# Five edits to an adaLN, long-convolution and SwiGLU block: norm rows at the gate, five-step statistics, paced spectrum loads, 100-column matmuls, 64-row pairs in the last row block

## The chip, the core and the metric

The kernel runs on one core of a Trainium2 chip. The metric is device time in microseconds (us) of one launch, lower is better; runs are compared by their median. Engines are named as in the profile: PE (matmuls) and PEld (its weight loads), DVE (vector), ACT (scalar), POOL (GpSimd), SP (the queue that issues nearly all DMAs).

## What is computed

Sequence 2048, width 576, hidden width 4608, everything stored in bf16. Six modulation rows come from one conditioning row. A first layernorm of `q` is modulated and multiplied by a long convolution of `k_shift * v` along the sequence; the result goes back onto the residual. A second layernorm feeds a SwiGLU.

```
mod = silu(c) @ w_mod                      # sa, ca, ga, sb, cb, gb
h   = layernorm(q) * (1 + ca) + sa
kv  = (4-tap shift of k) * v
y   = fftconv(kv, ssm_k)[:2048] + kv * ssm_D
x   = q + ga * (h * y)
h   = layernorm(x) * (1 + cb) + sb
out = x + gb * ((silu(h @ w1) * (h @ w3)) @ w2)
```

## The kernel before, in words

**Tiling.** The sequence is cut into 8 blocks of 256 rows (`s`, two rows to a partition) for the convolution, and into 4 row blocks of 512 rows (`r`) for the SwiGLU. The convolution of a block is done with short spectra: `x_spectrum(s)` makes the spectrum X of block s from `kv` (matmuls, copied out of PSUM by ACT), `w_spectrum` and `v_block` make the filter spectra V, and `pair(X, V, s)` multiplies two of them into an accumulator on DVE (L405 for the first, L410 and L412 for the others, each on 128x3456 elements). Later blocks need pairs with all earlier X and V; those that no longer fit are spilled to DRAM and fetched again by `get` (L430 to L434; three buffers for X, four for V). `inverse` (L539) turns the accumulator back into rows, `residual` adds it, and `outcome` makes the second norm. `turn_all` (L571) transposes the rows into `h2T`, the operand of the SwiGLU.

**First norm.** `gate_stats(s)` lets ACT make sums and sums of squares (L440, a Copy and a Square, each with an accumulator read), and `ln_scales` (L450 to L461) turns them into a scale and a shift with six small POOL operations: L455 mean, L456 variance term, L457 mean squared, L458 difference, L459 power -0.5, L460 shift. `gate_rows(s)` (L493 to L502) is two ACT activations of 128x576 that write `hg`, the normed rows; `gate(s)` is the modulation of `hg` on DVE (L511, L513). In `conv(s0)`, which handles blocks s0 and s0+1, `gate_rows(s0)` stands ahead of `x_spectrum(s0)`, and `gate(s0)` comes at the end of what runs beside that spectrum (`beside`): `v_block(s1)`, `load_kv(s1)`, `gate_stats(s1)`, up to two pairs, then the gate.

**SwiGLU.** `stream(r, ...)` runs over 36 tiles f of 128 hidden columns, in 9 chunks `fc` of four. For each f there are a gate product (w1) and an up product (w3) over 576 = 4*128 + 64 rows: eight matmuls of 128 rows (L916) and two of 64 rows (L927), one for w1 on partitions 0 to 63 and one for w3 on 64 to 127, issued side by side. ACT then applies Silu (L935) and copies the up product (L937), DVE multiplies them into `h3` (L938). Tiles are grouped by two, in the last row block by four, so that the 64-row matmuls of a group stand together. `load_w13` (L867 the 512 KB slabs, L868 the 64 KB ones) fills one of two buffers. `down(r)` multiplies `h3` with w2 (L982, loads at L973), DVE scales and adds to the residual (L999, L1000).

**Order.** The convolution of blocks 2r+2 and 2r+3 is a generator whose steps carry a cost; `advance` takes steps while `stream` and `down` of row block r are written out, so that DVE works on the convolution beside PE's SwiGLU. The instructions are then ordered within each engine by a scheduler that takes what it thinks is ready, in order of priority, unless an edge fixes the order. `behind(engine)` is such an edge: what is traced inside it is issued after the engine's last instruction so far. `get` has none. The first block is written out by hand (`first_block`, with `in_order` for DVE, ACT and PE). There `mod_columns` (L248) makes the columns of cb and sb with 60 matmuls of one output column each, and `warm` (L626) runs matmuls whose result nobody reads.

Of the kernel before, what the change touches and what calls it, by code (L numbers as in the profile page):

```python
# [2 lines left out]

# [19 lines left out]
NF = F // P  # L23
RB = 512
NRB = S // RB
FC = 4
# [6 lines left out]
N1 = 24  # L33
SPLIT = 2
EPS = 1e-5


def _ap(t, offset, dims):
# [5 lines left out]
class _Kernel:  # L44
    def __init__(self, ctx, tc, q, k, v, shift_k, ssm_k, ssm_D, w1, w3, w2, c, w_mod, out):
        self.tc, self.nc = tc, tc.nc
        self.q, self.k, self.v = q, k, v
        self.shift_k, self.ssm_k, self.ssm_D = shift_k, ssm_k, ssm_D
        self.w1, self.w3, self.w2, self.c, self.w_mod, self.out = w1, w3, w2, c, w_mod, out
        pool = lambda name, **kw: ctx.enter_context(tc.tile_pool(name=name, **kw))  # L50
        self.const = pool("const", bufs=1)
        self.psum = pool("psum", bufs=4, space=bass.MemoryType.PSUM)
        self.dram = pool("spill", bufs=1, space=bass.MemoryType.DRAM)
        self.spec = pool("spec", bufs=4)
        self.wprev = pool("wprev", bufs=2)
        self.prod = pool("prod", bufs=1)
        self.acc = pool("acc", bufs=1)
        self.ld = pool("ld", bufs=1)
        self.kvp = pool("kvp", bufs=1)
        self.x1p = pool("x1p", bufs=4)  # L60
        self.lnp = pool("lnp", bufs=1)
        self.small = pool("small", bufs=4)
        self.hp = pool("hp", bufs=4)
        self.xo, self.hg, self.accs, self.l1 = {}, {}, {}, {}
        self.X, self.V, self.Wl = {}, {}, {}
        self.w13, self.kept = {}, {}

    def ps(self, shape=(P, 2, 512), dtype=F32):
        return self.psum.tile(list(shape), dtype, name="ps", tag="ps")
# [2 lines left out]
    def setup(self):  # L72
        nc, const = self.nc, self.const
        nc.scalar.preload_act_table(ACT.Silu)
        self.ident = const.tile([P, P], BF16, name="ident")
        self.npi = const.tile([P, 1], F32, name="npi")
# [159 lines left out]
    def mod_columns(self):  # L236

        nc = self.nc
        w5 = self.wm[:, 0:5 * 6 * D].rearrange("p (a d) -> p a d", a=5)
        ps = self.ps()  # L240
        for i, m in enumerate((4, 3)):
            for j in range(6):
                lo = min(P * j, 512)
                n = P if j < 4 else 64
                out = ps[0:n, i, j:j + 1] if j < 5 else ps[64:P, i, 4:5]
                for ct in range(5):
                    k = P if ct < 4 else 64
                    nc.tensor.matmul(out, w5[0:k, ct, m * D + lo:m * D + lo + n],  # L248
                                     self.crep[0:k, ct, 0:1], start=(ct == 0), stop=(ct == 4))
        nc.scalar.activation(self.cbcol[:], ps[:, 0, 0:5], ACT.Copy, bias=1.0)  # L250
        nc.scalar.copy(self.sbcol[:], ps[:, 1, 0:5])


    def load_kv(self, s, between=None):
# [175 lines left out]
    def get(self, which, i):  # L430
        t = self.spec.tile([P, 6, D], BF16, name=which, tag=which, bufs=3 if which == "X" else 4)
        src = self.Xd if which == "X" else self.Vd
        self.nc.sync.dma_start(t[:].rearrange("p a d -> p (a d)"), src[i])
        return t  # L434

    def ln_sums(self, src, i, ssum, ssq, col=None):
        col = i if col is None else col
        for func, out in ((ACT.Copy, ssum), (ACT.Square, ssq)):
            junk = self.lnp.tile([P, D], BF16, name="junk", tag="junk")
            self.nc.scalar.activation(junk[:], src[:, i, :], func, accum_out=out[:, col:col + 1])  # L440

    def ln_stats(self, src, name):

# [6 lines left out]
    def ln_scales(self, ssum, ssq, name):  # L450
        small = self.small
        n = ssum.shape[-1]
        mean, var, rstd, nmr = [small.tile([P, n], F32, name=name + k, tag=f"ln{k}{n}") for k in "mvrn"]
        e = self.nc.gpsimd
        e.tensor_single_scalar(mean[:], ssum[:], -1.0 / D, op=ALU.mult)  # L455
        e.tensor_scalar(var[:], ssq[:], 1.0 / D, EPS, op0=ALU.mult, op1=ALU.add)  # L456
        e.tensor_mul(rstd[:], mean[:], mean[:])  # L457
        e.tensor_sub(var[:], var[:], rstd[:])  # L458
        e.tensor_tensor(rstd[:], var[:], self.neghalf[:, 0:n], op=ALU.pow)  # L459
        e.tensor_mul(nmr[:], mean[:], rstd[:])  # L460
        return rstd, nmr  # L461

    def quick_stats(self, src, name):
# [329 lines left out]
    def conv(self, s0):  # L793
# [24 lines left out]
            if s0 == 2:  # L818
                yield from self.pair(self.X[0], self.V[s0], s0)
        yield from self.mix(filters(), old())  # L820
        self.gate_rows(s0)
        X0, V0 = self.old_x(0, s0), self.old_v(0, s0)

        def beside():
            yield from self.v_block(s1)
            with self.behind(self.nc.sync):
                self.load_kv(s1)
            yield from self.gate_stats(s1)
            if s0 > 2:
                yield from self.pair(X0, self.V[s0], s0)  # L830
            self.X1 = self.old_x(1, s0)
            yield from self.pair(X0, self.V[s1], s1)
            yield from self.gate(s0)
        yield from self.mix(self.x_spectrum(s0), beside())
        yield from self.x_sums(s0)
# [45 lines left out]
    def stream(self, r, jobs, rate, size, finish=False):  # L881
# [64 lines left out]
        for k in range(0, len(items), size):  # L946
# [13 lines left out]
            for m in late:  # L960
                full(m, False)
                hide(m)

    def down(self, r, rate):
        nc = self.nc
        for h in range(2):
# [4 lines left out]
            for f0 in range(0, NF, W2C):  # L971
                w = _ap(self.w2m, (h * NF + f0) // W2C % NW2 * W2C * H, [[H, W2C], [1, H]])
# [8 lines left out]
                for f, t in order:  # L981
                    nc.tensor.matmul(acc[t],  # L982
                                     self.h3[:, f0 + f, t * P:(t + 1) * P], w[:, f, :],
                                     start=(f0 + f == 0), stop=(f0 + f == NF - 1))
# [51 lines left out]
    def row_blocks(self, n1):  # L1036
        for r in range(NRB):
            cost = 0
            if r + 1 < NRB:
                s0 = 2 * r + 2  # L1040
# [4 lines left out]
            rate = cost / time  # L1045
# [9 lines left out]
            else:  # L1055
                spills = {1: (self.keep_x, 1), 2: (self.keep_v, 0), 4: (self.keep_v, 1)} if r == 1 else {}
                jobs = [(fc, 0, RB, (r + fc) % 2, (lambda f, i: lambda: f(i))(*spills[fc]) if fc in spills else None)
                        for fc in range(NF // FC)]
            self.stream(r, jobs, rate, 4 if r == NRB - 1 else 2)
            self.down(r, rate)  # L1060
            self.end()

# [52 lines left out]
```

## Time and profile before

| | |
|---|---|
| median of 4 runs | 519.52 us (518.03 to 520.07) |
| the profiled execution, its own time | 516.79 us |
| its span, first to last instruction | 514.6 us |
| PE / DVE / ACT / POOL busy | 495.6 / 340.8 / 292.6 / 58.4 us |
| chain of work that ended last | PE 63%, DVE 23%, ACT 6%, issue 3%, POOL 2%, DMA 2% |
| matmuls L916, L982, L927 busy | 263.4, 145.4, 42.7 us |
| pairs on DVE, L410 and L412 | 28 each, 1956 and 1957 ns |
| DMA moved | 107.76 MB, 209 GB/s over the span |
| mean granted PE clock | 0.997 |

The stages, read from the timeline: first block to 31.7 us; convolution of blocks 1 to 3 beside the first row block to about 134; its `down` (from 131) to 167; row block 1 to 245.6 and its `down` to about 288; row block 2 to 367 and its `down` to 403.6; row block 3, with no convolution beside it, to 475.4; the last `down` to the end. The span is shorter than the profiled execution's own time by what lies before the first and after the last instruction, here 2.2 us.

### The profile page before, as it was taken

The page shows a single profiled execution, that of the slowest core. Times are in us where ns is not written, and L with a number is a line of the kernel's source. Part 1 is how long each engine was busy: PE and PEld are TensorE (multiplying, and loading weights), DVE is VectorE, ACT ScalarE, POOL GpSimd, SP SyncE. Part 2 cuts the span into 40 slices and gives each one's busy share as a digit, 9 for nine tenths or more (in the row PEclk, how much of TensorE's full clock was granted, in tenths as well). Part 3 has the DMA queues.
Part 4 walks back from the last instruction along what each step waited for, and adds up shares of the span by engine and source line. Part 5 has one row for each costly group of instructions (what it writes and reads, how often), then busy time and mean ns, then how long its engine had stood idle before and what let it go on. Part 6 is the DMA issues. An engine that isn't in the chain of part 4 may idle for free.

```text
span 514.6 us, 8602 instructions
## 1 busy us (share of the span) xinstructions
PE 495.6 (96%) x3334; PEld 293.0 (57%) x3362; DVE 340.8 (66%) x515; ACT 292.6 (57%) x581; POOL 58.4 (11%) x109
## 2 busy tenths in 40 slices
PE   7999988999999999999998999999999999999997
PEld 3767863557787444344776543434688544444775
DVE  8899898999993464997999984299660212112012
ACT  6668697578342569669453365966816345546000
POOL 3314023004040001102010000120101000000000
PEclk9999998999999999999999999999999999999999
DMA  8958966688979757558999763645455454550462
GB/s 285 334 153 238 316 212 204 188 261 267 308 236 354 239 174 242 173 166 316 344 331 355 274 195 117 200 147 179 138 139 142 146 174 128 157 174 2 119 181 70
DMA packets 102204, 107.76 MB, mean 209 GB/s; under 512 B 5075, under 2 KB 94228, under 8 KB 102164
## 3 DMA queue, kind: packets, MB, share of 16 engines
q1 hardware_dynamic: 102142, 107.21, 66.4%
q8 instruction: 26, 0.43, 0.3%
q14 instruction: 14, 0.11, 0.1%
q10 hardware_dynamic: 22, 0.01, 0.0%
HBM read 96.00 MB, written 11.21 MB: 208 GB/s over the span
## 4 chain that ended last, share of the span: by engine, by line
PE 63%; DVE 23%; ACT 6%; issue 3%; POOL 2%; DMA 2%; SPq 0%; POOLq 0%; DVEq 0%; ACTq 0%
PE ps L916 36%; PE ps L982 18%; PE ps L927 5%; DVE p L410 5%; DVE z L412 3%; DVE h L938 2%; DMA wst<-in_B_w_dram 1%; PE ps L313 1%; DVE kvt L334 1%; ACT junk L440 1%; DVE kv L335 1%; PE ps L539 1%; DVE z L405 1%; DMA knat<-in_A_ssm_k_dram 1%; ACT X L302 1%
## 5 line engine op out<-in xcount | busy, mean ns | idle before, releaser
L916 PE MATMUL ps<-h2T,wst 128*128 128x512 bf16 (+1 forms) x1317 | 263.4, 350 | 2.7 <-ACT W L315 0.8
L916 PEld LDWEIGHTS <-wst 128*128 128x128 bf16 x1344 | 128.0, 98 | 122.3 <-issue 19.7
L935 ACT ACTIVATE h<-ps 128x512 bf16<-128x512 f32 x144 | 87.0, 604 | 108.4 <-PE ps L927 71.0
L982 PE MATMUL ps<-wst,h 128*128 128x288 bf16 x1152 | 145.4, 286 | 3.3 <-DMA wst<-in_B_w_dram 2.5
L982 PEld LDWEIGHTS <-h 128*128 128x128 bf16 x1152 | 112.3, 98 | 33.0 <-issue 3.8
L938 DVE TENSOR_TENSOR h<-h,u 128x512 bf16<-128x512 bf16 x144 | 60.6, 424 | 95.6 <-ACT u L937 95.4
L937 ACT CAST u<-ps 128x512 bf16<-128x512 f32 x144 | 84.8, 589 | 0.0
L410 DVE TENSOR_TENSOR p<-X,V 128x3456 bf16<-128x3456 bf16 x28 | 54.8, 1956 | 5.3 <-DMA X<-Xd 5.1
L412 DVE TENSOR_TENSOR z<-z,p 128x3456 bf16<-128x3456 bf16 x28 | 54.8, 1957 | 0.2
L999 DVE TENSOR_TENSOR og<-ps,gbrow 128x288 bf16<-128x288 f32 x32 | 13.2, 452 | 48.8 <-PE ps L982 48.8
L927 PE MATMUL ps<-h2T,wst 64*128 64x512 bf16 (+1 forms) x336 | 42.7, 351 | 2.4 <-ACT X L315 2.1
L440 ACT ACTIVATE junk<-x 128x576 bf16<-128x576 bf16 x54 | 37.6, 696 | 0.5
L601 ACT ACTIVATE h2T<-ps,sbcol,cbcol 128x256 bf16<-128x256 bf16 x35 | 16.8, 571 | 24.9 <-PE ps L571 24.9
L927 PEld LDWEIGHTS <-wst 64*128 64x128 bf16 x336 | 11.4, 94 | 29.2 <-issue 26.4
L455 POOL TENSOR_SCALAR l2m<-l2s 128x2 f32<-128x2 f32 x6 | 9.3, 1544 | 154.3 <-ACT junk L440 154.3
L455 POOL TENSOR_SCALAR l1m<-l1s 128x2 f32<-128x2 f32 x7 | 8.6, 1223 | 139.0 <-ACT junk L440 139.0
L566 ACT ACTIVATE h2row<-x,l2n,l2r 128x576 bf16<-128x576 bf16 (+1 forms) x24 | 13.8, 653 | 13.6 <-POOL l2n L460 13.6
L334 DVE TENSOR_TENSOR kvt<-kh,shk 128x1152 bf16<-128x1152 bf16 x24 | 18.1, 755 | 3.4 <-DMA kh<-in_A_k_dram 3.3
L335 DVE TENSOR_TENSOR kv<-kv,kvt 128x1152 bf16<-128x1152 bf16 x24 | 18.1, 756 | 0.3
L315 ACT CAST X<-ps 128x576 bf16<-128x576 f32 x24 | 15.6, 659 | 0.0
L745 ACT CAST y<-ps 128x576 bf16<-128x576 f32 x14 | 8.5, 652 | 11.1 <-PE ps L539 11.1
L405 DVE TENSOR_TENSOR z<-X,V 128x3456 bf16<-128x3456 bf16 x7 | 13.7, 1956 | 1.4 <-DMA X<-Xd 1.4
(137 smaller groups left out, 356.3 us busy)
## 6 DMA issues: line engine op xcount, KB each, us to landing
wst<-in_B_w_dram SPq DMA_DIRECT2D x80, 512.0 KB, 4.9
wst<-in_B_w_dram SPq DMA_DIRECT2D x72, 288.0 KB, 4.2
X<-Xd SPq DMA_DIRECT2D x8, 864.0 KB, 5.4
Xd<-X SPq DMA_DIRECT2D x6, 864.0 KB, 5.9
wst<-in_B_w_dram SPq DMA_DIRECT2D x80, 64.0 KB, 3.0
kh<-in_A_k_dram SPq DMA_DIRECT2D x7, 720.0 KB, 7.8
Vd<-V SPq DMA_DIRECT2D x4, 864.0 KB
V<-Vd SPq DMA_DIRECT2D x4, 864.0 KB
```

Source lines behind the costliest of these rows:

```text
L334: nc.vector.tensor_mul(tmp[:], kh[:, 3 - j:5 - j, :], tap(j))
L335: nc.vector.tensor_add(kv[:], kv[:], tmp[:])
L405: nc.vector.tensor_mul(self.accs[s][:], X[:], V[:])
L410: nc.vector.tensor_mul(p[:], X[:], V[:])
L412: nc.vector.tensor_add(z[:], z[:], p[:])
L440: self.nc.scalar.activation(junk[:], src[:, i, :], func, accum_out=out[:, col:col + 1])
L916: nc.tensor.matmul(gus[k][:, i, a * n:(a + 1) * n], w[:, 5 * i + ct, (fi + a) * P:(fi + a + 1) * P], hT[:, ct, t0:t1], start=(first and ct ...
L927: nc.tensor.matmul(gus[k][:, i, a * n:(a + 1) * n], w[rows, 4, (fi + a) * P:(fi + a + 1) * P], hT[rows, 4, t0:t1], start=(first and a == 0 ...
L935: nc.scalar.activation(h3, gus[k][:, 0, :].rearrange("p (a t) -> p a t", a=m), ACT.Silu)
L937: nc.scalar.copy(u[:], gus[k][:, 1, :])
L938: nc.vector.tensor_mul(h3, h3, u[:].rearrange("p (a t) -> p a t", a=m))
L982: nc.tensor.matmul(acc[t], self.h3[:, f0 + f, t * P:(t + 1) * P], w[:, f, :], start=(f0 + f == 0), stop=(f0 + f == NF - 1))
```

## The change

The edits, in the order of the source: (1) `mod_columns` writes 100 equal output columns per matmul instead of one and reads every hundredth. (2) From the seventh call on, `get` issues its DMA behind SP's last instruction so far. (3) The factors 1/D go into the ACT sums, and `ln_scales` has five POOL operations. (4) `gate_rows(s0)` moves from ahead of `x_spectrum(s0)` to just ahead of `gate(s0)`. (5) The last row block uses `stream_halves`: every product is cut into 64-row matmuls, issued in pairs, one on partitions 0 to 63 and one on 64 to 127. In a tile's first part the lower half works for w1 and the upper for w3 (five pairs, the 64 leftover rows among them), in its second part the other way round (four pairs). Between the two parts of a tile stands the first part of the next. Since the two halves write the same PSUM bank one after the other, the second part waits for a POOL `memset` of one element that itself waits for the last matmul of the first part.

```
 mod_columns
-                out = ps[0:n, i, j:j + 1] if j < 5 else ps[64:P, i, 4:5]
+                out = ps[0:n, i, 100 * j:100 * (j + 1)] if j < 5 else ps[64:P, i, 400:500]
...
-                                     self.crep[0:k, ct, 0:1], start=(ct == 0), stop=(ct == 4))
+                                     self.crep[0:k, ct, 0:100], start=(ct == 0), stop=(ct == 4))
...
 get                                                       # EARLY_GETS = 6
-        self.nc.sync.dma_start(t[:].rearrange("p a d -> p (a d)"), src[i])
+        self.gets += 1
+        with self.behind(self.nc.sync) if self.gets > EARLY_GETS else nullcontext():
+            self.nc.sync.dma_start(t[:].rearrange("p a d -> p (a d)"), src[i])
 ln_sums
-        for func, out in ((ACT.Copy, ssum), (ACT.Square, ssq)):
+        for func, scale, out in ((ACT.Copy, -1.0 / D, ssum), (ACT.Square, D ** -0.5, ssq)):
...
 ln_scales
-        e.tensor_single_scalar(mean[:], ssum[:], -1.0 / D, op=ALU.mult)
-        e.tensor_scalar(var[:], ssq[:], 1.0 / D, EPS, op0=ALU.mult, op1=ALU.add)
-        e.tensor_mul(rstd[:], mean[:], mean[:])
-        e.tensor_sub(var[:], var[:], rstd[:])
+        e.tensor_mul(var[:], ssum[:], ssum[:])
+        e.tensor_sub(var[:], ssq[:], var[:])
+        e.tensor_single_scalar(var[:], var[:], EPS, op=ALU.add)
         e.tensor_tensor(rstd[:], var[:], self.neghalf[:, 0:n], op=ALU.pow)
-        e.tensor_mul(nmr[:], mean[:], rstd[:])
+        e.tensor_mul(nmr[:], ssum[:], rstd[:])
 conv
         yield from self.mix(filters(), old())
-        self.gate_rows(s0)
...
             yield from self.pair(X0, self.V[s1], s1)
+            self.gate_rows(s0)
             yield from self.gate(s0)
 row_blocks
-            self.stream(r, jobs, rate, 4 if r == NRB - 1 else 2)
+            if r == NRB - 1:
+                self.stream_halves(r)
+            else:
+                self.stream(r, jobs, rate, 2)
+    def stream_halves(self, r):
...
+        def part(f, swap):
+            w = ws[f // FC]
+            cols = slice(f % FC * P, (f % FC + 1) * P)
+            for ct in range(4 if swap else 5):
+                for rows, i in ((slice(0, 64), swap), (slice(64, P), 1 - swap)):
+                    nc.tensor.matmul(gus[f][:, i, :], w[rows, 5 * i + ct if ct < 4 else 4, cols], hT[rows, ct, :],
+                                     start=swap == 0 and ct == 0, stop=swap == 1 and ct == 3)
+                    if swap == 1 and ct == 0 and i == 1:
+                        self.wait_for(newest(), marks.pop(f))
+            if swap == 0:
+                first = newest()
+                nc.gpsimd.memset(self.tok[:], 0.0)
+                marks[f] = newest()
+                self.wait_for(marks[f], first)
...
+        for f in range(NF + 1):
+            if f < NF:
+                if f % FC == 0:
+                    self.load_w13(f // FC, (r + f // FC) % 2)
+                    ws[f // FC] = self.w13.pop(f // FC)
+                gus[f] = self.ps()
+                part(f, 0)
+            if f > 0:
+                part(f - 1, 1)
+                hide(f - 1)
```

More of the change, by code (lines that the diff above doesn't have):

```diff
@@ L1 @@
-from contextlib import ExitStack
+from contextlib import ExitStack, nullcontext
 import math
@@ L35 @@
 EPS = 1e-5
+EARLY_GETS = 6
 def _ap(t, offset, dims):
@@ L66, in __init__ @@
         self.w13, self.kept = {}, {}
+        self.gets = 0
     def ps(self, shape=(P, 2, 512), dtype=F32):
@@ L75, in setup @@
         self.ident = const.tile([P, P], BF16, name="ident")
+        self.tok = const.tile([1, 1], F32, name="tok")
         self.npi = const.tile([P, 1], F32, name="npi")
@@ L248, in mod_columns @@
                     nc.tensor.matmul(out, w5[0:k, ct, m * D + lo:m * D + lo + n],
-                                     self.crep[0:k, ct, 0:1], start=(ct == 0), stop=(ct == 4))
-        nc.scalar.activation(self.cbcol[:], ps[:, 0, 0:5], ACT.Copy, bias=1.0)
-        nc.scalar.copy(self.sbcol[:], ps[:, 1, 0:5])
+                                     self.crep[0:k, ct, 0:100], start=(ct == 0), stop=(ct == 4))
+        nc.scalar.activation(self.cbcol[:], ps[:, 0, 0:500:100], ACT.Copy, bias=1.0)
+        nc.scalar.copy(self.sbcol[:], ps[:, 1, 0:500:100])
     def load_kv(self, s, between=None):
@@ L437, in ln_sums @@
         col = i if col is None else col
-        for func, out in ((ACT.Copy, ssum), (ACT.Square, ssq)):
+        for func, scale, out in ((ACT.Copy, -1.0 / D, ssum), (ACT.Square, D ** -0.5, ssq)):
             junk = self.lnp.tile([P, D], BF16, name="junk", tag="junk")
-            self.nc.scalar.activation(junk[:], src[:, i, :], func, accum_out=out[:, col:col + 1])
+            self.nc.scalar.activation(junk[:], src[:, i, :], func, scale=scale, accum_out=out[:, col:col + 1])
     def ln_stats(self, src, name):
@@ L452, in ln_scales @@
         n = ssum.shape[-1]
-        mean, var, rstd, nmr = [small.tile([P, n], F32, name=name + k, tag=f"ln{k}{n}") for k in "mvrn"]
+        var, rstd, nmr = [small.tile([P, n], F32, name=name + k, tag=f"ln{k}{n}") for k in "vrn"]
         e = self.nc.gpsimd
-        e.tensor_single_scalar(mean[:], ssum[:], -1.0 / D, op=ALU.mult)
-        e.tensor_scalar(var[:], ssq[:], 1.0 / D, EPS, op0=ALU.mult, op1=ALU.add)
-        e.tensor_mul(rstd[:], mean[:], mean[:])
-        e.tensor_sub(var[:], var[:], rstd[:])
+        e.tensor_mul(var[:], ssum[:], ssum[:])
+        e.tensor_sub(var[:], ssq[:], var[:])
+        e.tensor_single_scalar(var[:], var[:], EPS, op=ALU.add)
         e.tensor_tensor(rstd[:], var[:], self.neghalf[:, 0:n], op=ALU.pow)
-        e.tensor_mul(nmr[:], mean[:], rstd[:])
+        e.tensor_mul(nmr[:], ssum[:], rstd[:])
         return rstd, nmr
@@ L962, in stream, with wait_for, hide @@
                 hide(m)
+    def wait_for(self, later, first):
+        self.tc.add_manual_dep(
+            later, first.name,
+            mybir.DependencyInfo(mybir.DependencyClass.Sync, mybir.DependencyReason.DATA),
+            reason="both halves of the rows write this bank, one after the other")
+    def stream_halves(self, r):
+        nc = self.nc
+        hT = self.h2T[r % 2]
+        newest = lambda: nc.cur_bb.bb.instructions[-1]
+        gus, ws, marks = {}, {}, {}
+        def part(f, swap):
[12 more added lines that the diff above has]
+                self.wait_for(marks[f], first)
+        def hide(f):
+            h3 = self.h3[:, f, :]
+            nc.scalar.activation(h3, gus[f][:, 0, :], ACT.Silu)
+            u = self.hp.tile([P, RB], BF16, name="u", tag="u")
+            nc.scalar.copy(u[:], gus.pop(f)[:, 1, :])
+            nc.vector.tensor_mul(h3, h3, u[:])
+        for f in range(NF + 1):
[8 more added lines that the diff above has]
+                hide(f - 1)
     def down(self, r, rate):
```

## The prediction

> **What bounds the kernel now.** I read the page's 40 slices first, then busy times by stage, then idle gaps of PE and DVE in the timeline. In the slices of the page (12.9 us each) DVE is full in the first twelve and again in the 17th to 24th; PE is full nearly everywhere, and its clock is granted in full but for the 7th.
>
> ```profile
> PE   7999988999999999999998999999999999999997
> DVE  8899898999993464997999984299660212112012
> PEclk9999998999999999999999999999999999999999
> DMA  8958966688979757558999763645455454550462
> ```
>
> By stage (length; PE, PEld, DVE, ACT, POOL busy with counts; clock, DMA share, GB/s):
>
> ```profile
> 31.70:134.70 103.00, 97.49 (x777) 65.61 (x778) 97.43 (x140) 75.76 (x151) 21.85 (x26) 0.98 0.75 232
> 240.00:289.00 49.00, 47.00 (x373) 34.39 (x372) 48.39 (x52) 22.20 (x44) 5.19 (x10) 1.00 1.00 346
> 312.00:334.00 22.00, 21.80 (x110) 8.90 (x110) 6.09 (x14) 16.76 (x36) 1.71 (x6) 1.00 0.53 163
> 403.60:475.40 71.80, 71.17 (x354) 30.22 (x360) 16.48 (x42) 36.74 (x70) 0.00 (x0) 1.00 0.43 131
> ```
>
> From 31.7 to 134.7 DVE sets the end: 97.4 of 103 us, 5.6 idle. From 240 to 289 PE and DVE are level, and the DMA engines are full (share 1.00). From 289 PE alone counts. So a microsecond is worth something on DVE early, on either (with the DMAs) in row block 1's down pass, on PE after that.
>
> **Edit 5, the last row block.** Here all is PE. The timeline of PE, then of the weight loads inside one burst of 64-row matmuls:
>
> ```profile
> 407.13 1.04 PE L927 MATMUL ps<-h2T,wst 64*128 64x512 bf16 x8
> 408.10 7.08 PE L916 MATMUL ps<-h2T,wst 128*128 128x512 bf16 x31
> 415.12 1.04 PE L927 MATMUL ps<-h2T,wst 64*128 64x512 bf16 x8
> ...
> 407.36 0.10 PEld L927 LDWEIGHTS <-wst 64*128 64x128 bf16 x2
> 407.58 0.10 PEld L927 LDWEIGHTS <-wst 64*128 64x128 bf16 x2
> ```
>
> A group of four tiles takes 415.12 - 407.13 = 7.98 us: 32 matmuls of 128 rows and 4 pairs of 64. Inside a burst a pair's two loads take 0.10 us together and the next pair's come 0.22 us later (0.216 unrounded), the pitch of one full matmul (0.216: 32 take 6.9 us). So two halves cost one slot, and a group needs 36 * 0.216 = 7.78 us after; the 0.20 us that goes is the change of row mode in and out. Nine groups save 1.8; one change of mode and the shift at the ends remain, so -1.65 (ends: -0.5 at a pitch of 0.220, -1.9).
>
> The new wait: the second part of a tile waits for POOL, with all of PE's queue behind it, and ACT's Silu (L935) behind that. Between lie five pairs of the next tile, 1.08 us, less the 0.16 that a matmul's 0.38 us outlasts its slot: 0.92 us of cover. The round trip is some 0.08 us to POOL (DVE to POOL in the first block), 0.10 for a memset (128x1 at the start), perhaps 0.43 behind one DVE multiply (L938), 0.04 back: 0.65. POOL has nothing else there (0.00 busy). I take 0. The chunk's two 512 KB loads now wait for its last tile's second part, 1.1 us later and both at once; the page's median landing is 4.9 us and a chunk takes 7.8, so 7.8 - 1.1 - 4.9 = 1.8 us are left, less some 0.4 for SP's issue. A landing above 6.3 us would show as a stall.
>
> [...]
>
> **Edit 4, gate rows.** Two ACT activations (0.87 us each) move behind the spectrum's four copies, `gate_stats(s1)`'s eight ACT instructions and one or two pairs. In blocks 2 and 3:
>
> ```profile
> 79.39 0.40 POOL L460 TENSOR_TENSOR l1n<-l1m,l1r 128x2 f32<-128x2 f32 x1
> 79.82 1.62 ACT L500 ACTIVATE hg<-x,l1n,l1r 128x576 bf16<-128x576 bf16 x2 [2.92 <-POOL l1n L460]
> 81.47 0.76 DVE L511 TENSOR_TENSOR hg<-hg,arow 128x1152 bf16<-128x1152 bf16 x1 [1.07 <-ACT hg L500]
> 82.01 0.61 PE L927 MATMUL ps<-h2T,wst 64*128 64x512 bf16 x2 [2.14 <-ACT X L315]
> ```
>
> ACT stands 2.92 us for POOL, so PSUM is not emptied, PE stands 2.14, and the PE clock is halved for the next 3.4 us (full-width matmuls start 0.43 us apart until 85.5). PE recovers some 4 us, but DVE sets the end, and it stood 1.07 us here and 0.67 at 88.8 for a matmul that came late: 1.74 to be had. Part of the 1.07 may come back at the gate's new place, where DVE again follows two activations. I take -1.3 (ends 0 and -1.9, DVE's idle time from 76 to 89.5). In later blocks the move lies in PE's shadow. What is late next: DVE's own work, without a gap from 89.5 to 134.7.
>
> **Edit 1, 100 columns.** PE in the first block:
>
> ```profile
> 22.16 3.72 PE L248 MATMUL ps<-crep,h 128*128 128x1 bf16 x60
> 25.82 2.13 PE L299 MATMUL ps<-kT,Fk 128*128 128x288 bf16 x16
> 27.79 1.46 PE L626 MATMUL ps<-shk,ident 128*128 128x512 bf16 x5
> 29.75 0.45 PE L578 MATMUL ps<-ident,h2row 128*128 128x128 bf16 x5 [0.51 <-DVE h2row L477]
> ```
>
> Matmuls of one column start 25 ns apart, transposes of 128 columns (L364) 56 ns; 100 columns are then 44. Of each five, all differ by about 19 ns or, at the two changes of row mode, by 30 to 40: 0.12 us in twelve fives, +1.5 us. PE's order is fixed here: 25.82 becomes 27.3, the six warming matmuls end at 30.6 instead of 29.1, and the transposes L578 start then instead of at 29.75. Everything behind them (ACT's and DVE's writes of h2T, then DVE's convolution) starts 0.8 later: +0.8 (ends 0, if the streams hide under loads of 0.096 us, and +1.5).
>
> **Edit 3, five steps.** One POOL operation fewer, 0.2 to 0.6 us. After the squares arrive, four remain as before, so only a crowded POOL gains. In the first block hg (21.07) may come up to 0.7 earlier, but then L578 waits for PE, see above. 0 (ends -0.7 and 0).
>
> **Edit 2, paced loads.** Six of twelve fetches (V2, X5, V1, X0, V0, X1 for blocks 6 and 7; 864 KB each) are issued today as soon as a buffer is free; five of them between 261 and 280 us, into the full DMA engines. PE's down pass pays:
>
> ```profile
> 266.96 6.05 PE L982 MATMUL ps<-wst,h 128*128 128x288 bf16 x48 [0.34 <-DMA wst<-in_B_w_dram]
> 274.63 6.04 PE L982 MATMUL ps<-wst,h 128*128 128x288 bf16 x48 [1.61 <-DMA wst<-in_B_w_dram]
> 289.62 0.72 PE L364 MATMUL ps<-ident,knat 128*128 128x128 bf16 x10 [0.25 <-DVE og L999]
> ```
>
> Paced, they go out behind w1/w3 loads of row block 2. Each tile of row block 2 advances the generator by 2.05 * 108 / 93.5 = 2.37 units; V2 comes after 24.7 units, in tile 10, so behind chunk 2's load (issued at 296 today); in the same way X5 and V1 follow chunk 3 (305), X0 and V0 chunk 4 (313). The 4.4 MB that leave the 49 us lower 346 GB/s to some 256. PE's 1.95 us of waits go; the 0.25 shows DVE just as late, but one pair there (284.9 to 288.8) uses V2 and moves away with it. Later DVE has room: idle 15.9 of 22 us from 312 to 334, against three moved pairs of 3.9. -2.0 (ends 0 and -2.2).
>
> **Sum.** -1.65 - 1.3 + 0.8 + 0 - 2.0 = -4.15 us: the profiled execution would go from 516.79 to about 512.6 (span 510.5), and, since the median of the runs is 2.7 above it, the median from 519.52 to 515.4. All ends together give 512.8 to 520.5.
>
> **Rivals.**
> - The change does only part of what it says, and only the last row block gains (14%). The scheduler, not the source, places instructions: if the gate's wait comes back elsewhere and DVE still has the old pairs ahead of L999, edits 2 and 4 give nothing: -1.65 + 0.8, 518.7. For it: L511 waits 1.07 behind L500 at four places; against it: the 5 us of PE that edit 4 frees.
> - Slower, by the token (7%). POOL's first operation after a wait takes 0.2 to 4.7 us (L455). That was beside a full DVE; here DVE is at 23%. If the memset and its hand-overs exceed 0.92 us, all 35 tiles pay the excess: at L455's mean of 1.2 us, 0.4 * 35 = +14, 530 us. It turns the sign above 1.0 us.
> - Fetches too late (7%). If SP's queue holds them a chunk longer, the moved pairs run into block 6's spectrum sums (338) and row block 3 waits: -1.65 - 1.3 + 0.8 + 5 = +2.9, 522.4.
>
> The forecast has 70%; 2% are for what I do not see. The range, 512.8 to 519.8, holds the forecast with the ends of its terms, but for the corner where all are at their worst, and the first rival. About 0.3% (1.6 us) is what a measurement of this kernel can tell from no change. The forecast is faster by more than that but for a small part, the first rival lies within it, the others beyond: faster 0.69, within 0.16, slower 0.15.
>
> **What would show it.** Right: one row mode from 403 to 475 and a stage near 70.1 us; no L500 wait for POOL near 80 and no half clock there; L248 at about 5.2 us and L578 near 30.6; no DMA wait of PE near 274, V fetches after 296. Wrong: PE waiting for POOL each 2 us, a pair pitch above 0.22, DVE idle near 82 as before, PE waits for DVE after 338.

## The result

| | before | after |
|---|---|---|
| median | 518.41 us (516.51 to 520.95, 50 runs) | 520.54 us (517.83 to 522.23, 31 runs) |
| profiled execution's span | 514.6 us | 518.2 us |
| PE / DVE / POOL busy | 495.6 / 340.8 / 58.4 us | 497.3 / 340.0 / 72.1 us |
| PE's down pass of row block 1, first matmul's start to last one's | 245.6 to 286.8 us | 251.9 to 290.9 us |

The ratio is 1.0039, with a 95% interval of 1.0029 to 1.0050: 2 us slower, where 4 us faster was forecast. POOL has fewer operations in each norm and is busy 14 us longer, of which the 36 memsets of edit 5 make only 3.2; that row of the page is the first hint. (Ratios and their intervals leave out executions far above the fastest of the same kernel, which matters only for the two runs of edit 2 alone, where three of twelve and one of eight are left out.)

### The profile page after: what moved, and what is told of

It reads as the page before. It is cut to its first block, busy times and chain, and to the rows that moved or that the text cites. A ratio compares the mean times of both kernels' runs of the same rounds, so it can differ in the third digit from the quotient of the medians.

```text
span 518.2 us, 9246 instructions
## 1 busy us (share of the span) xinstructions
PE 497.3 (96%) x3630; PEld 295.5 (57%) x3650; DVE 340.0 (66%) x515; ACT 293.8 (57%) x581; POOL 72.1 (14%) x131
## 4 chain that ended last, share of the span: by engine, by line
PE 70%; DVE 20%; ACT 4%; POOL 2%; issue 2%; DMA 1%; SPq 0%; DVEq 0%; ACTq 0%
PE ps L1032 27%; PE ps L920 20%; PE ps L987 12%; PE ps L931 3%; DVE p L413 2%; DVE z L415 2%; DVE h L942 2%; DVE kv L338 2%; DVE kvt L337 2%; POOL l2v L460 2%; PE ps L543 2%; DMA wst<-in_B_w_dram 1%; PE ps L316 1%; ACT junk L445 1%; PE ps L251 1%
## 5 line engine op out<-in xcount | busy, mean ns | idle before, releaser
L920 PE MATMUL ps<-h2T,wst 128*128 128x512 bf16 (+1 forms) x1037 | 199.0, 340 | 2.1 <-ACT W L318 0.8
L920 PEld LDWEIGHTS <-wst 128*128 128x128 bf16 x1056 | 100.2, 98 | 85.8 <-issue 14.2
L942 DVE TENSOR_TENSOR h<-h,u 128x512 bf16<-128x512 bf16 x108 | 45.2, 423 | 43.2 <-ACT u L941 43.2
L987 PE MATMUL ps<-h2T,wst 64*128 64x512 bf16 x648 | 70.3, 376 | 0.3 <-DMA wst<-in_B_w_dram 0.3
L413 DVE TENSOR_TENSOR p<-X,V 128x3456 bf16<-128x3456 bf16 x28 | 54.8, 1957 | 6.9 <-DMA X<-Xd 4.3
L987 PEld LDWEIGHTS <-wst 64*128 64x128 bf16 x648 | 31.3, 94 | 39.0 <-DMA wst<-in_B_w_dram 1.4
L1049 DVE TENSOR_TENSOR og<-ps,gbrow 128x288 bf16<-128x288 f32 x32 | 13.2, 454 | 48.8 <-PE ps L1032 48.8
L460 POOL TENSOR_TENSOR l2v<-l2s 128x2 f32<-128x2 f32 x6 | 14.3, 2382 | 155.1 <-ACT junk L445 155.1
L460 POOL TENSOR_TENSOR l1v<-l1s 128x2 f32<-128x2 f32 x7 | 18.1, 2581 | 126.4 <-ACT junk L445 126.4
L931 PE MATMUL ps<-h2T,wst 64*128 64x512 bf16 (+1 forms) x264 | 33.1, 342 | 0.3
L570 ACT ACTIVATE h2row<-x,l2n,l2r 128x576 bf16<-128x576 bf16 (+1 forms) x24 | 13.8, 653 | 17.0 <-POOL l2n L464 17.0
L931 PEld LDWEIGHTS <-wst 64*128 64x128 bf16 x264 | 8.5, 94 | 21.1 <-issue 20.8
```

Source lines behind the costliest of these rows:

```text
L413: nc.vector.tensor_mul(p[:], X[:], V[:])
L460: e.tensor_mul(var[:], ssum[:], ssum[:])
L920: nc.tensor.matmul(gus[k][:, i, a * n:(a + 1) * n], w[:, 5 * i + ct, (fi + a) * P:(fi + a + 1) * P], hT[:, ct, t0:t1], start=(first and ct ...
L931: nc.tensor.matmul(gus[k][:, i, a * n:(a + 1) * n], w[rows, 4, (fi + a) * P:(fi + a + 1) * P], hT[rows, 4, t0:t1], start=(first and a == 0 ...
L942: nc.vector.tensor_mul(h3, h3, u[:].rearrange("p (a t) -> p a t", a=m))
L987: nc.tensor.matmul(gus[f][:, i, :], w[rows, 5 * i + ct if ct < 4 else 4, cols], hT[rows, ct, :], start=swap == 0 and ct == 0, stop=swap == ...
```

## The profile after

The slices of the page (13.0 us each):

```profile
PE   7998989989799999999999999999999999999996
DVE  8897799998797336798999736999661222222012
POOL 3304005207003001100102000540101000000000
PEclk9998999999899999999999999999999999999999
```

PEclk is the clock granted to PE, in tenths of full speed. Its dip in the seventh slice before (at PE's wait near 82 us, which edit 4 was to remove) is gone. Two others are new, in the fourth slice (39 to 52 us) and in the eleventh (130 to 143), and PE and DVE have a 7 in the eleventh. By stage, with the columns of the prediction's table; the first two stretches begin and end at the same work as there:

```profile
32.60:141.40 108.80, 98.31 (x771) 65.97 (x773) 96.54 (x137) 75.76 (x150) 26.83 (x22) 0.97 0.71 217
246.40:295.40 49.00, 48.95 (x390) 35.68 (x390) 47.07 (x58) 24.22 (x47) 4.92 (x9) 1.00 0.88 278
312.00:334.00 22.00, 21.80 (x108) 8.83 (x109) 18.51 (x21) 14.17 (x31) 4.70 (x1) 1.00 0.96 337
408.00:478.70 70.70, 70.39 (x651) 31.30 (x648) 16.21 (x41) 37.23 (x70) 3.17 (x36) 1.00 0.44 134
```

The late stages went about as forecast. The stretch around row block 1's down pass moves 278 GB/s instead of 346 and PE stands 0.05 us in it instead of 2.0; the moved pairs fill DVE from 312 to 334 (18.5 us instead of 6.1); the last row block takes 70.7 instead of 72.0 us. But for the 0.9 us by which it begins later, all that was lost lies in the first line: 108.8 us where 103.0 stood, with DVE idle for 12.3 us instead of 5.6. It has two places. The first, PE in block 0 and block 1:

```profile
22.14 5.31 PE L251 MATMUL ps<-crep,h 128*128 128x100 bf16 x60
30.65 0.44 PE L582 MATMUL ps<-ident,h2row 128*128 128x128 bf16 x5
43.53 2.89 PE L302 MATMUL ps<-kv,Fb 128*128 128x288 bf16 x16 [2.03 <-DVE kv L340]
46.22 2.43 PE L222 MATMUL ps<-wst,crep 128*128 128x288 bf16 x10
```

The 100 columns cost what was said: 5.31 us instead of 3.72, the transposes 0.9 later. But then PE waits 2.03 us for kv, and its clock is halved for a while (0.50 from 45.0 to 46.5): the sixteen matmuls of L302 take 2.89 us (2.13 at full clock in block 0). DVE, behind PE's results, then stands 3.41 us ahead of L354 at 47.13.

The second place, POOL, then ACT and PE (start, length, operation; in brackets the wait before it):

```profile
119.49 8.21 POOL L460 TENSOR_TENSOR l2v<-l2s 128x2 f32<-128x2 f32 x1 [25.81 <-ACT junk L445]
127.78 0.19 POOL L461 TENSOR_TENSOR l2v<-l2q,l2v 128x2 f32<-128x2 f32 x1
...
129.39 0.87 ACT L570 ACTIVATE h2row<-x,l2n,l2r 128x576 bf16<-128x576 bf16 x1 [6.36 <-POOL l2n L464]
...
132.67 0.72 PE L367 MATMUL ps<-ident,knat 128*128 128x128 bf16 x10 [4.29 <-ACT u L941]
```

An operation on 128x2 elements takes 8.21 us; the next takes 0.19. It is the first step of block 2's second norm. ACT needs that norm for L570, stands 6.36 us, empties no PSUM, and PE stands 4.29. Such a long stay of a small POOL operation is called a hold below. Before, the first step of the same norm took 2.63, and PE stood 0.24 at the same matmuls (lines of before):

```profile
116.59 2.63 POOL L455 TENSOR_SCALAR l2m<-l2s 128x2 f32<-128x2 f32 x1 [26.20 <-ACT junk L440]
...
125.99 0.72 PE L364 MATMUL ps<-ident,knat 128*128 128x128 bf16 x10 [0.24 <-ACT u L937]
```

DVE in the two kernels at that place, after first:

```profile
122.34 0.77 DVE L338 TENSOR_TENSOR kv<-kv,kvt 128x1152 bf16<-128x1152 bf16 x1
123.00 0.44 DVE L942 TENSOR_TENSOR h<-h,u 128x512 bf16<-128x512 bf16 x1
123.34 0.77 DVE L321 TENSOR_TENSOR X<-X 128x1152 bf16<-128x1152 bf16 x1
```
```profile
118.38 0.76 DVE L334 TENSOR_TENSOR kvt<-kh,shk 128x1152 bf16<-128x1152 bf16 x1
119.17 0.76 DVE L335 TENSOR_TENSOR kv<-kv,kvt 128x1152 bf16<-128x1152 bf16 x1
```

After, each operation starts about 0.1 us before the one ahead of it ends (122.34 + 0.77 is later than 123.00): the scheduler has interleaved independent work, and the row is so from the hold's start to 127.6. Before, L335 needs the `kvt` of L334 right ahead of it, starts 34 ns after L334's end (unrounded), and POOL's L455 ends within 0.1 us of that, at 116.59 + 2.63 = 119.22. Unrounded, DVE has only two gaps between 89.5 and 134.7 in the trace of before, of 34 ns each, this one and one at 89.53. That gives two explanations. (a) Edit 3 is to blame: the norm's first step has two operands now. (b) **While DVE runs two-input operations without a gap, a small POOL operation can be kept out (8.21 us here); edit 4 changed DVE's order and took the gap away.** The expectations of the first runs hold (a) for the theory and (b) for its rival; beside both stands edit 1's wait near 43.5.

## The experiments

Each ran beside the kernel before on the same chip. Line numbers are those of after, or one higher behind an added line.

**The edits one by one.** In these five runs one edit of the diff above is made and the other four are left out. Edit 1:

> The kernel before with edit 1 alone (100 columns). Theory: the edit costs twice, 0.65 us because PE is late for the first transposes, and some 3.6 us because the scheduler then places a first pair (128x3456) on DVE ahead of the last steps of kv_rows(1), for which PE's spectrum of block 1 waits: a PE wait of about 2 us near 43, the PE clock halved after it, +4.2 us in all, 522.6 against a median before of 518.4. Rival: the edit costs its PE time alone, +0.7, 519.1, and the PE wait near 43 is the work of another edit.

Measured 521.11 us against 518.52, ratio 1.0061 (1.0038 to 1.0084). DVE, then PE:

```profile
39.76 1.95 DVE L408 TENSOR_TENSOR z<-X,V 128x3456 bf16<-128x3456 bf16 x1
41.97 0.74 DVE L338 TENSOR_TENSOR kv<-kv,kvt 128x1152 bf16<-128x1152 bf16 x1
42.97 0.75 DVE L340 TENSOR_TENSOR kv<-kv,vt 128x1152 bf16<-128x1152 bf16 x1
```
```profile
43.86 2.12 PE L302 MATMUL ps<-kv,Fb 128*128 128x288 bf16 x16 [2.02 <-DVE kv L340]
```

PE waits 2.02 us for L340, as in after; the clock stays full behind it in this trace, against the theory. Edit 1 costs about 2.6 by the medians, not 0.8, and less than the theory's 4.2. Edit 2:

> The kernel before with edit 2 alone (paced fetches). Theory: the waits of PE for w2 near 267 and 274 go and nothing comes in their place: -2.2 us, 516.2; the down pass of row block 1 falls from 41.2 to about 39. Rival: the gain in the profile after belongs to the shifted start of that pass, and this run stays at 518.4.

Measured 522.41, in two groups: four executions from 516.4 to 518.0, eight from 521.9 to 527.9. The traced one is short: PE's waits near 267 and 274 are gone, and the down pass takes 39.0 us instead of 41.2. Neither the theory nor the rival foresaw the long ones; they are taken up below. Edit 3:

> The kernel before with edit 3 alone (five steps). Theory: the first POOL operation, now one with two tensor operands, is held up while DVE works without a gap, longer than the one with a single operand was; ACT waits for the statistics in its order, PE behind it: one such wait of 5 us or more before 134 and +2 to +4 us, 521. Rival: what holds POOL is only the order on DVE, which all edits together make; alone this edit moves the time by less than 0.7 us, 518.4.

Measured 518.58, ratio 1.0002 (0.9984 to 1.0021): it does nothing that shows. The step with two operands is held no longer than the old one, and explanation (a) falls:

```profile
117.22 2.62 POOL L460 TENSOR_TENSOR l2v<-l2s 128x2 f32<-128x2 f32 x1 [25.18 <-ACT junk L445]
```

Edit 4:

> The kernel before with edit 4 alone (gate rows at the gate). Theory: the wait of ACT for POOL near 77 and PE's stall near 82 go, -1.6 us, 516.8, and no half clock near 82. Rival: the moved rows change the order on DVE so that the second norm's POOL chain near 117 is held for 8 us, as in the profile after: +2 us, 520.4.

Measured 523.13, ratio 1.0100 (1.0070 to 1.0130). Edit 4 by itself brings the hold, with the old single-operand step. The rival, (b), is right in that; what the gap does is tested further down.

```profile
115.85 8.23 POOL L460 TENSOR_SCALAR l2m<-l2s 128x2 f32<-128x2 f32 x1 [25.15 <-ACT junk L445]
```

Edit 5:

> Edit 5 alone. Theory: the last row block loses its eighteen changes of row mode and nothing else changes, so row block 3 takes 70.7 us instead of 72.0 and the time falls by 1.2 to 1.3 us, to about 517.2; PE waits for POOL nowhere in it. Rival: the memset's round trip costs something that the trace of all five edits hides, and the time stays at 518.5 or above.

Measured 517.91 against 518.60; the ratio, 0.9996 (0.9974 to 1.0018), cannot tell 1.2 us from nothing. The trace can: row block 3 takes 70.5 us instead of 72.0, and PE never waits for POOL in it.

**Edit 1 with DVE's order put back.**

```
 conv_second
         yield from self.kv_rows(1)
+        kv = [i for i in self.nc.cur_bb.bb.instructions if i.engine == self.nc.vector.engine][-1]
         yield from self.v_block(1)
-        yield from self.pair(self.X[0], self.V[1], 1)
+        with self.tc.issue_after(kv): yield from self.pair(self.X[0], self.V[1], 1)
```

> Edit 1 alone, with one order added: block 1's first pair is issued behind the last kv operation of block 1, as in the kernel before. Theory: edit 1's cost has two parts, +0.7 us on PE in the first block and +1.9 us from the order on DVE that the scheduler changed; with the order put back the PE wait of 2.0 us near 43.9 for kv is gone, the half clock after it too, and about 519.2 is left. Rival: the 0.7 us themselves make PE or DVE late there, the wait stays and the time is about 521.1.

Measured 518.35, ratio 0.9997 (0.9977 to 1.0016). The pair now follows kv, and the wait is gone:

```profile
40.57 0.75 DVE L340 TENSOR_TENSOR kv<-kv,vt 128x1152 bf16<-128x1152 bf16 x1
41.76 1.95 DVE L408 TENSOR_TENSOR z<-X,V 128x3456 bf16<-128x3456 bf16 x1
```
```profile
41.46 2.12 PE L302 MATMUL ps<-kv,Fb 128*128 128x288 bf16 x16
```

So nearly all that edit 1 cost came from the order: the scheduler had put the pair L408 (1.95 us on DVE) ahead of the last two kv steps. The 0.8 us of PE itself does not show at the end, but the interval reaches 0.8 too. One thing stays open: of edit 1's traced execution, 1.7 us lie elsewhere, in row block 1's down pass, where PE waits 2.16 us for w2 and then runs 48 matmuls in 7.71 us instead of 6.04; how many executions had that is not known. Two runs further down, in which edit 2 has taken that wait away, also differ by 2.6 us in the order alone.

**Edit 4 with a gap made on DVE.** At each second norm of a later block DVE gets one operation that reads POOL's variance:

```
 ln_scales
-        e.tensor_sub(var[:], var[:], rstd[:])
+        e.tensor_sub(var[:], var[:], rstd[:]); self.touch(var, name)
...
+    def touch(self, t, name):
+        if name == "l2":
+            seen = self.small.tile([P, 2], F32, name="seen", tag="seen")
+            self.nc.vector.tensor_scalar_add(seen[:], t[:], 1.0)
```

> Edit 4 alone, with one small DVE operation added at the second norm of each later block: it reads the variance that POOL has just made (128x2), so DVE stands still until POOL has got that far. Theory: POOL's first operation of that norm is held as long as DVE leaves no gap; here it ends within 2.5 us instead of 8.23, DVE stands about 0.8 us at three to six places, ACT's wait of 6.5 and PE's of 4.4 near 129 are gone, and edit 4 then gains its 1.3 to 1.6 less about 0.9: 517.5 to 518.5, against 523.1 without the added operation. Rival: the hold has nothing to do with DVE's gaps, POOL takes its 8 us, DVE now waits for it, and the time is 523 or more.

Measured 517.37, ratio 0.9987 (0.9961 to 1.0013), and 523.13 without the operation. POOL, then DVE:

```profile
117.16 2.34 POOL L460 TENSOR_SCALAR l2m<-l2s 128x2 f32<-128x2 f32 x1 [25.16 <-ACT junk L445]
119.58 0.20 POOL L462 TENSOR_TENSOR l2r<-l2m 128x2 f32<-128x2 f32 x1
```
```profile
118.65 0.77 DVE L337 TENSOR_TENSOR kvt<-kh,shk 128x1152 bf16<-128x1152 bf16 x1
120.24 0.17 DVE L1119 TENSOR_SCALAR seen<-l2v 128x2 f32<-128x2 f32 x1 [0.83 <-POOL l2v L462]
```

DVE's row of work ends at 118.65 + 0.77 = 119.42, DVE waits 0.83 us, and POOL's first step ends at 119.50, then three steps in 0.7 us. DVE's other operations stand in the same order here as in edit 4 alone (L517, L334, L942, L337, then L320 and L338), so it is the wait that makes the difference. The control, in which that order is the same again, is two operations on DVE that wait for nobody; the scheduler puts one other operation between them:

```
 outcome
-                    r, b = self.ln_stats(self.xo[s], "l2")
+                    r, b = self.ln_stats(self.xo[s], "l2"); self.gap()
...
+    def gap(self):                                  # self.last: ssq of ln_stats
+        t = [self.small.tile([P, 2], F32, name="gap" + k, tag="gap" + k) for k in "ab"]
+        self.nc.vector.tensor_scalar_add(t[0][:], self.last[:], 1.0)
+        self.nc.vector.tensor_scalar_add(t[1][:], t[0][:], 1.0)
```

> Edit 4 alone, with two small DVE operations (128x2 each) at every second norm, the first on ACT's sums, the second on the first's result with another operation between: they wait for nothing that is late and leave no gap. Theory: only a gap on DVE lets POOL go, so POOL's first operation near 116 is held some 8 us as without them and the time stays at 522 to 524. Rival: any small or single-operand operation on DVE lets POOL in, the hold ends at the first of them, within 2 us, and the time is near 517.4.

Measured 522.08, ratio 1.0072 (1.0057 to 1.0087): the time follows the theory, the details only in part.

```profile
117.64 1.69 POOL L460 TENSOR_SCALAR l2m<-l2s 128x2 f32<-128x2 f32 x1 [25.15 <-ACT junk L445]
119.41 0.63 POOL L462 TENSOR_TENSOR l2r<-l2m 128x2 f32<-128x2 f32 x1
120.01 5.98 POOL L461 TENSOR_SCALAR l2v<-l2q 128x2 f32<-128x2 f32 x1
```

The first step ends at 119.33, beside `gapa` (119.16 to 119.35), which has one input: so far the rival was right. But then the third step is held for 5.98 us, though POOL had not waited before it, until DVE runs dry at 125.9. So it isn't only the first operation after a wait that can be held, and two one-input operations of 0.2 us on DVE did not keep POOL from being held here. The same addition to the kernel before shows what it costs by itself:

> The kernel before, none of the edits, with the small DVE operation at the second norms. Theory: before, DVE leaves a gap of 34 ns of its own 2.6 us after POOL's start near 116.6, so the operation brings nothing there and costs up to 0.8 us of DVE at two places: 518.5 to 520. Edit 4 with the operation (517.4) is then worth 1.1 to 2.6. Rival: the operation is worth more than a microsecond by itself, 517.4 or less, and edit 4 gives nothing even without the hold.

Measured 518.84 against 518.32, ratio 1.0011 (0.9993 to 1.0028): no gain of its own. Set against that, edit 4 (0.9987 with the operation) is worth some 1.2 us by the ratios, 1.8 by the medians, once POOL is not held near 117; the intervals overlap, so that gain is not shown.

**Together.** Edits 2 to 5 with the operation, first in the wrong place (on five-step `var` before its third step, which writes `var` again):

> Edits 2, 3, 4 and 5 without edit 1, with the same small DVE operation at the second norms. Theory: the gains add up as their sources lie in different stages, -1.2 in row block 3, -2.3 in row block 1's down pass less about 1 in row block 2, -0.7 net of edit 4: about 514.5. Rival: DVE sets the end up to 134 us and takes the gain of edit 4 back, and row block 2 takes back edit 2's: about 517.3, edit 5 alone.

Measured 520.38, ratio 1.0045 (1.0023 to 1.0067), 6 us above the theory. The trace shows the hold at a new place, POOL and then PE:

```profile
267.02 0.20 POOL L461 TENSOR_TENSOR l2v<-l2q,l2v 128x2 f32<-128x2 f32 x1
269.17 7.81 POOL L462 TENSOR_SCALAR l2v<-l2v 128x2 f32<-128x2 f32 x1 [1.96 <-DVE seen L1119]
```
```profile
281.90 0.72 PE L575 MATMUL ps<-ident,h2row 128*128 128x128 bf16 x5 [5.55 <-ACT h2row L570]
```

POOL must now wait until DVE has read `var`; when it may go on, DVE is in a row of pairs again. In after the same step took 0.22 us at 275.69. The operation moved one step on:

```
-        e.tensor_sub(var[:], ssq[:], var[:]); self.touch(var, name)
-        e.tensor_single_scalar(var[:], var[:], EPS, op=ALU.add)
+        e.tensor_sub(var[:], ssq[:], var[:])
+        e.tensor_single_scalar(var[:], var[:], EPS, op=ALU.add); self.touch(var, name)
```

> Edits 2, 3, 4 and 5 without edit 1, the small DVE operation moved one step: it now reads the variance after POOL's third operation, which POOL doesn't write again. Theory: the 7.8 us hold of POOL at 269.2 in the run before came from the wait that the small operation itself put on POOL, so it goes; row block 1's down pass takes about 39 us instead of 47.0, and the time is 520.4 less 6 to 8, about 513.5. Rival: the moved pairs of edit 2 make DVE full there in any case, POOL is held in its next operation, and the time stays above 517.

Measured 512.93 against 518.81, ratio 0.9898 (0.9875 to 0.9921). With all five edits, without and with the order of edit 1's experiment:

> All five edits, with the small DVE operation at the second norms as in the run beside it, and nothing else. Theory: of the 6.4 us by which the first row block's down pass ends late, the hold of POOL at 119.5 makes 4.3 to 5; it goes, PE's wait at 132.7 with it, and the time falls from 520.5 to about 516. What edit 1 costs through the order on DVE (PE's wait of 2.0 at 43.5) stays. Rival: DVE, not POOL, is late there, the small operation adds its own stalls, and the time stays near 520.

Measured 514.98, ratio 0.9932 (0.9908 to 0.9956).

> All five edits, the small DVE operation at the second norms, and block 1's first pair issued behind the last kv operation of block 1. Theory: both costs of the new orders are gone, what is left is what the prediction summed: -1.3 in row block 3, -2.3 in row block 1's down pass, -1.6 at the gate less 0.9 for the added operation, +0.7 for the 100 columns, +0.5 in row block 2's down pass: about -4, 514.5. Rival: the two costs share the same DVE time, so the order on DVE brings nothing more and the time equals that of the run with the small operation alone, about 516.

Measured 512.39, ratio 0.9881 (0.9863 to 0.9900): 6.4 us faster than before. PE at the place of after's wait at 132.67:

```profile
125.28 4.08 PE L1033 MATMUL ps<-wst,h 128*128 128x288 bf16 x32
```

(Lines are one higher here.) The down pass starts at 125.3 instead of 133.6. Against after's 520.54, measured on another occasion, the hold accounts for some 5.6 us and DVE's order in block 1 for 2.6.

**Edit 2.** Its worth: the fastest kernel with `EARLY_GETS = 99`, so that no `get` is paced:

> The fastest kernel so far (all five edits, the small DVE operation, the pair of block 1 behind the kv rows; 512.4) without edit 2. Theory: edit 2 is worth the 2.0 to 2.3 us that PE stood near 267 and 274 for weights, so 514.4 to 514.7. Rival: it is worth nothing in this company, since row block 2 takes back on DVE or ACT what the down pass gains: 512.4.

Measured 515.10 against 518.32, ratio 0.9941 (0.9928 to 0.9954), beside 0.9881 with edit 2: edit 2 is worth about 3 us here (2.7 by the medians). PE's wait is back:

```profile
274.08 2.12 PE L1033 MATMUL ps<-wst,h 128*128 128x288 bf16 x16 [1.71 <-DMA wst<-in_B_w_dram]
```

Then the long executions when edit 2 stands alone, first the same kernel again:

> Edit 2 alone, a second time, for a trace of its longer executions (8 of its 12 were 521.9 or more, 4 were 518 or less). Theory: in a long one POOL is held for some 5 us or more at the first norm of block 6, near 326, where ACT waits for the scale and shift at once; ACT does not empty PSUM, PE stands and its clock is halved, in row block 2. Rival: the long ones differ from the short ones in the first 130 us, or in DMA waits near 274, and edit 2 has no part in it.

Measured 523.36, only the traced execution at 518.88, the others from 522.4 up. In both runs the long ones have the lower mean clock (0.979 to 0.990, the short ones 0.992 to 0.997). The trace shows the threatened place in little: POOL's last step ends at 331.32, ACT's gate rows wait 2.27 us for it, PE stands 1.02 at 333.6.

```profile
331.36 1.63 ACT L504 ACTIVATE hg<-x,l1n,l1r 128x576 bf16<-128x576 bf16 x2 [2.27 <-POOL l1n L464]
```

Edit 2, and edit 4 for block 6 only:

```
 conv
-        self.gate_rows(s0)
+        s0 == 6 or self.gate_rows(s0)
...
             yield from self.pair(X0, self.V[s1], s1)
+            if s0 == 6: self.gate_rows(s0)
             yield from self.gate(s0)
```

> Edit 2 alone, and of edit 4 only what concerns block 6: ACT's two gate rows of that block come after the spectrum. Theory: the long executions of edit 2 alone come from POOL being held at block 6's first norm while ACT waits for it; here ACT doesn't wait, so all executions lie near the short ones, 516 to 519, the median near 517. Rival: the long executions have their cause in the first 130 us or in the transfers, and the median stays at 522 or more.

Measured 515.65 (514.86 to 517.46) against 518.32, ratio 0.9959 (0.9943 to 0.9974). With block 6's gate rows moved, none of the seven executions is long. So the long ones need block 6's gate rows ahead of the spectrum, where ACT waits for POOL. That POOL is held there for some 5 us in them was not seen, since no long one was traced.

## Why the prediction failed, step by step

Two steps of it failed and made the loss: the one of edit 4, with some 5.6 us in after, and the one of edit 1, with 2.6. The rest brought more than was forecast.

- **Edit 4, -1.3.** The wait it named is gone: no half clock near 82, and freed of the hold it gains perhaps that (1.2, not clear of the noise). The step that failed is "What is late next: DVE's own work, without a gap from 89.5 to 134.7". The missing gap was read as a mere full engine. There was one gap at the place that counts, the 34 ns at 119.14 at which POOL got through; edit 4 took it away, and POOL was held (8.23 us in edit 4 alone). The trace of before showed the price: L455 at 2.63 us in the place in question, 4.7 at most. The prediction used that row for the token, where DVE has gaps, and not for the second norm, where ACT and PE wait behind it. Worth: -1.3 expected, about +4.6 measured alone.
- **Edit 1, +0.8.** PE's 1.6 us and the 0.9 at the transposes came as worked out. "Everything behind them starts 0.8 later" failed: the scheduler, given other times, ordered DVE anew, and kv came after a pair. 2.6 measured alone, 0 with the order put back.
- **Edit 2, -2.0.** Right in place and sign: the fetches left the down pass, its waits went (268.9 to 284.6 runs through in after), the pairs moved to where DVE was idle. Worth about 3. "Later DVE has room" left out POOL: beside the fuller DVE (18.5 us busy of 22 instead of 6.1) the first step of block 6's first norm takes 8.82 us in after, 0.22 before; alone, edit 2 seems to pay for it at block 6. In after edit 4 shields that place: POOL is held at 329.30 and neither ACT nor PE waits for it.
- **Edit 3, 0.** Right within the interval, which is 2 us wide.
- **Edit 5, -1.65.** Right in mechanism; 1.2 to 1.7 in seven traces (stages of 70.3 to 70.8 us against 72.0, from the last down matmul of row block 2 to the first of row block 3). The last row block:

```profile
408.20 4.06 PE L987 MATMUL ps<-h2T,wst 64*128 64x512 bf16 x36
409.07 0.96 PEld L987 LDWEIGHTS <-wst 64*128 64x128 bf16 x10
409.52 0.09 POOL L993 MEMSET tok<- 1x1 f32 x1 [12.24 <-PE ps L987]
```

  Eighteen pairs take 4.06 us, 18 * 0.216 = 3.9 and the tail of the last; ten weight loads within 0.96 us are five pairs at that pitch (4 * 0.216 + 0.10). A pair's loads (0.09 us each) start 0.22 us behind the start of the pair ahead, whose matmuls take 0.38 us by the trace, and the pitch stays 0.216: the loads add no time that shows. The memset takes 0.09 us each time, and PE never waits for it; the token rival was wrong. In after one late load adds 0.31 us, at 431.1.
- **A cost put at nothing:** "In later blocks the move lies in PE's shadow" is short of 0.5 us. Row block 2's down pass takes 38.4 instead of 37.9 us in every kernel with block 6's gate rows moved (PE waits 1.03 us for ACT in it instead of 0.48).
- **The rivals.** The first had the right ground ("the scheduler, not the source, places instructions") but priced it as a gain not had. None held a new wait in the first 134 us, so the range ended at 519.8.
- **The sum.** With both losses taken out, the five edits bring 6.4 us, more than the 4.15 of the forecast. The worths found one by one (3 for edit 2, 1.2 each for edits 4 and 5) make 5.4 of it; the rest is not assigned.

## What to carry to other kernels

When an edit moves work under a scheduler, compare the order on every engine, not only where the moved instruction lands: both losses here came from instructions that the diff doesn't touch. Where a small POOL operation lies on another engine's path, look at what DVE runs beside it, and whether any of it waits; a short DVE operation that reads POOL's result was a cheap way to force a gap here (0.5 us by the medians in the kernel before, though DVE waited 6.7 us for it at three places), but POOL must not wait for it in turn. And of several edits, those that look worthless in sum may be good ones beside a bad one: edit 2 gains some 3 us here, edit 5 and perhaps edit 4 about 1 each.

## What the runs showed of the hardware

- A POOL operation of 0.2 us took up to 8.8 us while DVE ran two-input operations in SBUF without a gap (8.21, 8.23, 7.81, 5.98 and 8.82 us, for example). The first four ended at a gap of 34 ns or more, or where DVE ran dry; the fifth ended between two multiplications that overlap by 23 ns, where the others in its row overlap by some 90. Others ended where DVE waited (at 119.50 in edit 4 with the operation, 0.08 us into a DVE wait of 0.83), or beside a DVE operation with one input in SBUF (in after, L460 at 273.83 takes 1.50 us and ends beside L1049, 275.19, which reads PSUM; L460 of the control ends beside `gapa`). The hold of 8.21 us spans twelve DVE operations, from L517 (119.33) to L413 (to 127.65). No hold shows at the memset, which reads nothing: it took 0.09 us each of 36 times in after, 34 of them while a two-input operation (`h<-h,u`, 0.43 us, but for one) ran on DVE.
- What remains open: a gap is not always needed. In the chain of small operations the next ones mostly passed at the end of a single DVE operation (0.37 to 1.11 us each at 119.3 to 122.3 before), without a gap, while the third in the control was held for 5.98 us. A first step can pass so too: in the second run of edit 2 alone, POOL got in at the end of one pair operation, though DVE's next one started 0.09 us before that end. Which end lets POOL in, the runs don't settle.

```profile
325.62 1.85 POOL L460 TENSOR_SCALAR l1m<-l1s 128x2 f32<-128x2 f32 x1 [51.83 <-ACT junk L445]
```

- A PE wait of 2.0 us was followed by half the clock in one trace (L302 2.89 us, after 2.03 us) and by full clock in another (2.12 us with edit 1 alone, after 2.02 us). It was the same in the down pass: 48 matmuls took 7.71 us after a wait of 2.16 us (edit 1 alone, at 277.92) and 6.04 us after one of 2.13 (edit 4 alone, at 279.95). In the control, a wait of 2.02 us at 280.05 was followed by a mean clock of 0.70 from 280 to 283.
